# Where the 64-bit weight w_in is converted: in the first four chains, or beside the fifth chain and the first batch's V

## The chip, the cores and the metric

The kernel runs on one core of a Trainium2 chip. A core has five engines that follow instruction streams of their own and wait for one another by semaphores: TensorE (PE: matrix products, results in PSUM), VectorE (DVE), ScalarE (ACT), GpSimd (POOL) and SyncE (SP, which here only issues DMA transfers). Each engine works through its stream in order; a DMA is issued by one engine's queue and carried out by 16 DMA engines. The metric is the device time of one execution in microseconds (us).

## The reference

The reference has three stages on 4 batches of 768 positions. The first is a delta-rule attention with 8 heads of 48 channels; per head, with a 48x48 state:

```
y_t     = q_t @ state
state  += beta_t * outer(k_t, v_t - k_t @ state)      # k normalised
```

Its output x (4 x 768 x 384) goes through a gated MLP, in which w_in is float64:

```
h = gelu(x @ w_in);  u, v = h[..., :512], h[..., 512:]
v = w_sg @ layernorm(v) + b_sg                         # over positions
x = x + (u * v) @ w_out
```

and then through a token mixer and a channel MLP (two products with relu each, with w_tok1, w_tok2, w_ch1, w_ch2).

## The kernel before

**Stage one** (`phase_a`) turns the recurrence into blocks. It treats six groups g = 0..5, a group being two batches by a third of the positions. For each group there are these pieces:

- `kk(g)` and `qk(g)`: the products of keys with keys and queries with keys on TensorE (L159, L134), four units each. Their evictions go through ScalarE (L165, L169, L142); for g > 0 `kk` is then scattered into the tile MD by DMAs on SP's queue (L174, L175). GpSimd masks the query products (L145, L146).
- `solve(g)`: the inverse of a unit triangular matrix for 32 rows at a time, on VectorE: transpose MD into Li (L183), some scalars, 31 steps of a product and a sum (L209, L211), transposes into TD and TN (L214, L219). `tload` sends TD by four DMAs on SP's queue into the tile TW (L230).
- `merge(g)`: joins the blocks on TensorE with ScalarE evictions (L242 to L267). It waits for TW.
- `vput`: scaled values into YR on GpSimd (L273), which `chain` needs.
- `chain(g)`: the recurrence over four chunks c, four steps each, so 16 steps: `u` (L305), `d0`, `y0`, `y1` (L281, L291).

The order of instructions is written by hand. The six chains run one after the other; after each of a chain's 16 steps the table `ACT[g]` says what is put in: `S` advances solves, `K` and `Q` units of kk and qk, `m` units of merge, `l` the load of the next values, `v` the first `vput` of the next group, and `c` one step of a generator, `beside`, which converts w_in. Before the chains, the first solve runs through 31 steps `ns`, beside which ScalarE clears two AQ and one TW tile from the tile XZ (`zeros`, L108, L112): twelve pieces, four of them ahead of everything else, the rest from ns = 9 on.

**The conversion.** w_in arrives as pairs of 32-bit words. `load` works on tiles of 256 columns: a DMA on SP's queue into a tile `st` (L456); the square (`sq`, L468 on ScalarE or L469 on VectorE); four VectorE operations which build the float32 (`F`, L471, L472, L473, L476). `split` then makes a high and a low part, since the dense stages use three reduced-precision products in place of one float32 product (`mm3`, L547 to L549): a copy on ScalarE (L444), a subtraction on GpSimd (L445). With `out` given, the two parts are written to a DRAM buffer `scr` by two DMAs of GpSimd's queue (L487). Before, all 3072 columns (12 tiles) go this way while chains 0 to 2 run, with tiles of a pool of their own (`pcv`), which chain 3 gives back for the outputs xn of batches 2 and 3 (`room`).

**The dense stages** begin inside chain 5: its 16 steps each take one step of `pre`. `pre` loads the tile SA (named WIN) from `scr` by four DMAs on SP's queue (L699), transposes batch 0 (`trans`, L571 and L564), makes V (`V`, six blocks of 128 positions, evicted by gelu and layernorm, L577 to L593) and U (`U`, eight blocks). In this part two PSUM banks take turns, so a block's products wait until VectorE has read the block before the last one (L581). `start` sets up constants on GpSimd (L509 to L515). What is left of `pre` and the rest of the dense stages follow after chain 5.

Of the kernel before, what the change touches and what calls it, by code (L numbers as in the profile page):

```python
# [29 lines left out]
def phase_a(tc,I,xn,cfg,tail=None,beside=None,room=None):  # L30
    nc=cfg.get('wrap',lambda x:x)(tc.nc)
    es=ExitStack(); esE=ExitStack(); esP=ExitStack()
    with es:
# [80 lines left out]
        zs=zeros()  # L114
# [12 lines left out]
        def qk(g):  # L127
            for u in range(4):
# [7 lines left out]
                for par in range(2):  # L136
                    rr=T_[par]; q0=aq[rr,par].rearrange("p a c x -> p (a c) x")
                    if u in cfg['qd']:
                        nc.vector.tensor_tensor(q0,gp[rr],mask[rr].rearrange("p t x -> p (t x)").unsqueeze(1).to_broadcast([64,8,64]),ALU.mult)
                        continue  # L140
# [222 lines left out]
        for _ in range(4): next(zs)  # L363
# [7 lines left out]
        for ns in range(31):  # L371
# [4 lines left out]
            if ns>8: next(zs,0)  # L376
# [12 lines left out]
        vput(0,0)  # L389
        kt=[12]; mt=[8]  # L390
# [6 lines left out]
        for g in range(6):  # L397
# [4 lines left out]
            if g==3 and beside is not None:  # L402
                for _ in beside: pass
                room()
            if g==5 and tail is not None:
                while wait: tick()
                esP.close(); esE.close()
                fill=tail()
            for si,_ in enumerate(chain(g)):
                if fill is not None: next(fill,0)  # L410
                step[0]+=1; tick()
                for a in act[min(g,5)][si].split():
# [14 lines left out]
                    if a=='c' and beside is not None: next(beside,0)  # L427
# [6 lines left out]
def _dense(tc,I,O,xn,cfg):  # L434
# [11 lines left out]
    def load(src,hi,lo,parts,step=256,pool=None,ahead=2,g=1,out=None,lag=1):  # L446
# [33 lines left out]
        for i in range(0,n+lag*g,g):  # L480
            for j in range(max(i-lag*g,0),min(i-lag*g+g,n)):
                r=slice(todo[j][1],todo[j][1]+step)
                if out is None: split(Fs[j],hi[:,r],lo[:,r],True)
                else:
                    w=[pool.tile([128,step],F32R,name=n_,bufs=2) for n_ in ('sh','sl')]
                    split(Fs[j],w[0],w[1],True)
# [5 lines left out]
    def conv(PX,scr):  # L492

        yield from load(I['win'],None,None,[(0,3072,0)],pool=PX,lag=cfg.get('lag',1),g=cfg.get('cg',2),out=lambda r:(scr[0][:,r],scr[1][:,r]))
    me.conv=conv
    def start(scr):
# [199 lines left out]
        def pre():  # L696
            for h in (1,0):
                for i in range(2):
                    nc.sync.dma_start(R(WIN[i])[:,:,512*h:512*h+512],scr[i].rearrange("p (k f) -> p k f",f=1024)[:,:,512*h:512*h+512])  # L699
            yield from trans(0,XT)  # L700
            yield from V(0)
            yield from U(0)
# [84 lines left out]
def _row(ss,**k):  # L787

    r=[f'S{n}' if n else '' for n in ss]
    for a,at in k.items():  # L790
# [8 lines left out]
CFG={'nl':(0.5,0.2,0.7),'cg':2,'k0':(1,3,5,7),'q0':(11,13,15,17),'l1':20,'late':2,'far':3,'tl':2,'half':21,'hs':5,'qd':(),'act':ACT}  # L799
def build(tc,I,O,cfg):  # L800
    with tc.tile_pool(name="per",bufs=1,side="right") as pp, tc.tile_pool(name="scr",bufs=1,space=bass.MemoryType.DRAM) as pd, tc.manual_schedule():

        xn=[pp.tile([128,6,384],F32,name=f"xn{b}") for b in range(2)]
        d=_dense(tc,I,O,xn,cfg)
        scr=[pd.tile([128,3072],F32,name=f"scr{i}") for i in range(2)]
# [25 lines left out]
```

## Time and profile before

| | |
|---|---|
| median of 3 runs | 981.63 us (979.33 to 985.21) |
| profiled execution | 980.1 us, span 978.4 us |
| mean granted TensorE clock | 0.946 |
| PE busy | 856.8 us (88%) |
| DVE busy | 613.8 us (63%) |
| ACT busy | 391.2 us (40%) |
| POOL busy | 338.2 us (35%) |

A row of a timeline has the start and length in us, the engine, the line of the code, the instruction, its tiles (output <- inputs) and, in brackets, how long the engine had been idle before it and who released it. A row of the groups has the count, busy us, the mean ns of one, and idle time ahead. The chain of waits is followed back from the last instruction of the execution, and shown in order of time. DMA rows have the count, KB each and median us from issue to landing.

Stage one with the first steps of the dense stages takes the first third of the span (to about 340 us). The solves lie at 19 to 269 us, the chains at 78 to about 342, V of batch 0 at 308 to 330 on TensorE.

### The profile page before, as it was taken

The numbers are of one execution on the slowest core, as the hardware profiler recorded it, in microseconds if no ns is written. First come the engines' busy times: TensorE is split into PE (matmuls) and PEld (weight loads), VectorE is DVE, ScalarE is ACT, GpSimd is POOL, SyncE is SP. The second block draws the span as 40 slices with busy tenths as digits, with TensorE's granted clock in tenths as the row PEclk, the third lists the DMA queues.
The fourth block names the chain that finished last, engine by engine and source line by source line (L and its number), as shares of the span: only waits on it lengthen the run. The fifth ranks groups of instructions, "written<-read, shape, count | busy, mean of one in ns | idle before, by whom it ended". The sixth has DMA issues, their size and how long they took to land.

```text
span 978.4 us, 23130 instructions
## 1 busy us (share of the span) xinstructions
PE 856.8 (88%) x9644; PEld 812.9 (83%) x9644; DVE 613.8 (63%) x1254; ACT 391.2 (40%) x869; POOL 338.2 (35%) x434
## 2 busy tenths in 40 slices
PE   6456764878788899999999998989899999999998
PEld 4346764867787689999999987879899999999998
DVE  5999998989902787947839896878513213123122
ACT  4525543758787663423423432434212112112111
POOL 7330475777763534323234443834200000000000
PEclk9679776979999999999999997999999999999999
DMA  6564748675444040000000022224100000000000
GB/s 160 148 144 107 174 122 193 170 169 138 122 95 147 1 163 31 1 1 1 1 1 0 30 69 65 87 87 127 50 1 25 25 1 25 1 25 25 1 25 25
DMA packets 60344, 68.05 MB, mean 70 GB/s; under 512 B 30416, under 2 KB 37328, under 8 KB 60240
## 3 DMA queue, kind: packets, MB, share of 16 engines
q1 hardware_dynamic: 58288, 59.49, 23.3%
q0 software_dynamic: 1952, 7.08, 2.3%
q8 instruction: 76, 1.25, 0.5%
q14 instruction: 28, 0.23, 0.1%
HBM read 51.61 MB, written 7.86 MB: 61 GB/s over the span
## 4 chain that ended last, share of the span: by engine, by line
PE 65%; DVE 19%; ACT 4%; issue 4%; DMA 3%; POOL 2%; SPq 1%; DVEq 0%; ACTq 0%; POOLq 0%
PE ps L547 18%; PE ps L548 18%; PE ps L549 18%; DVE p L209 4%; DVE T L211 3%; DVE F L471 2%; DVE F L472 2%; DMA tw<-td 2%; PE yp L281 2%; PE gm L134 1%; PE gm L264 1%; PE ps L571 1%; DVE F L473 1%; PE ck L305 1%; PE gm L252 1%
## 5 line engine op out<-in xcount | busy, mean ns | idle before, releaser
L639 DVE SCALAR_TENSOR_TENSOR hlo<-ps,hh 128x384 fp32r<-128x384 f32 x96 | 53.5, 557 | 206.2 <-ACT hh L638 206.2
L638 ACT ACTIVATE hh<-ps 128x384 fp32r<-128x384 f32 x96 | 47.2, 491 | 227.1 <-PE ps L549 227.1
L547 PE MATMUL ps<-GU,SB 128*128 128x384 f32 x288 | 97.6, 339 | 0.0
L549 PE MATMUL ps<-GU,SB 128*128 128x384 f32 x288 | 97.5, 339 | 0.0
L548 PE MATMUL ps<-GU,SB 128*128 128x384 f32 x288 | 97.2, 338 | 0.0
L209 DVE TENSOR_TENSOR p<-Li,T 128x87 f32<-128x87 f32 (+15 forms) x186 | 81.2, 449 | 3.8
L211 DVE TENSOR_TENSOR T<-T,p 128x87 f32<-128x87 f32 (+15 forms) x186 | 74.2, 412 | 3.8
L548 PE MATMUL ps<-SB,VHt 128*128 128x384 f32 x192 | 65.0, 338 | 2.3 <-POOL SB L445 2.3
L549 PE MATMUL ps<-VHt,hlo 128*128 128x384 f32 x192 | 65.3, 340 | 1.3 <-DVE hlo L639 1.3
L547 PE MATMUL ps<-SB,VHt 128*128 128x384 f32 x192 | 65.0, 338 | 0.0
L547 PE MATMUL ps<-VHt,hh 128*128 128x384 f32 x192 | 65.0, 338 | 0.0
L548 PE MATMUL ps<-VHt,hh 128*128 128x384 f32 x192 | 64.6, 337 | 0.0
L549 PE MATMUL ps<-SB,VHt 128*128 128x384 f32 x192 | 64.5, 336 | 0.0
L614 POOL TENSOR_TENSOR q<-q,u 128x384 f32<-128x384 f32 x32 | 36.9, 1158 | 66.1 <-DVE q L613 66.1
L305 PE MATMUL ck<-yr,tw 128*64 128x48 f32 x768 | 38.1, 239 | 23.0 <-POOL yr L273 12.7
L273 POOL TENSOR_TENSOR yr<-v,nn 64x192 f32<-64x192 f32 x96 | 54.3, 566 | 9.0 <-DMA v<-in_vn_dram 2.2
L145 POOL TENSOR_SCALAR_AFFINE_SELECT aq<-aq 32x512 f32<-32x512 f32 x48 | 38.0, 791 | 55.6 <-ACT aq L142 50.7
L305 PEld LDWEIGHTS ck<-yr,tw 128*64 128x64 f32 x768 | 32.8, 151 | 26.8 <-POOL yr L273 14.7
L547 PE MATMUL ps<-X,SA 128*128 128x384 f32 x144 | 49.9, 346 | 5.8 <-DVE xn L626 3.2
L548 PEld LDWEIGHTS ps<-GU,SB 128*128 128x128 f32 x288 | 54.1, 188 | 0.9 <-DVE GU L564 0.9
L547 PEld LDWEIGHTS ps<-GU,SB 128*128 128x128 f32 x288 | 54.1, 188 | 0.6 <-DVE GU L564 0.6
L549 PEld LDWEIGHTS ps<-GU,SB 128*128 128x128 f32 x288 | 54.0, 188 | 0.3 <-POOL SB L445 0.3
(155 smaller groups left out, 2357.3 us busy)
## 6 DMA issues: line engine op xcount, KB each, us to landing
kq<-in_kq_dram SPq DMA_DIRECT2D x48, 256.0 KB, 4.3
st<-in_ch_dram SPq DMA_DIRECT2D x36, 256.0 KB, 2.8
aq<-in_qt_dram SPq DMA_DIRECT2D x24, 256.0 KB, 5.7
kn<-in_kn_dram SPq DMA_DIRECT2D x12, 384.0 KB, 7.0
out_dram<-xn SPq DMA_DIRECT2D x24, 192.0 KB, 1.9
v<-in_vn_dram POOLq DMA_DIRECT2D x10, 384.0 KB, 4.3
tw<-td SPq DMA_DIRECT2D x24, 128.0 KB, 4.3
st<-in_win_dram SPq DMA_DIRECT2D x12, 256.0 KB, 6.3
```

Source lines behind the costliest of these rows:

```text
L145: if blk==0: nc.gpsimd.affine_select(out=a,in_=a,pattern=[[0,8],[-64,2],[1,32]],compare_op=ALU.is_gt,fill=0.0,base=0,channel_multiplier=-1)
L209: nc.vector.tensor_tensor(p,Li[:,j,j+1:].unsqueeze(1).to_broadcast([128,w,n]),T[:,:w,j].unsqueeze(2).to_broadcast([128,w,n]),ALU.mult)
L211: nc.vector.tensor_tensor(T[:,:w,j+1:],T[:,:w,j+1:],p,ALU.add)
L273: n0=8*h+cc; nc.gpsimd.tensor_tensor(YRs[bb][gc%3][T_[par],:,par,:],VS[bb][T_[par],n0:n0+7:2,:],NNs[g%3][T_[par],16*bb+n0:16*bb+n0+7:2].un ...
L281: nc.tensor.matmul(yps[bb][o0:o0+64,2*pair+par,:],aq[F_,par,pair,cc,:],yr[F_,pair,par,:],start=True,stop=True)
L305: nc.tensor.matmul(u2[T_[par],pair,:],tw[F_,par,16*bb+8*h+2*pair+cc,:],yr[F_,pair,par,:],start=True,stop=True)
L547: nc.tensor.matmul(ps,L[0],Rr[0],start=first,stop=False)
L548: nc.tensor.matmul(ps,L[0],Rr[1],start=False,stop=False)
L549: nc.tensor.matmul(ps,L[1],Rr[0],start=False,stop=last)
L614: nc.gpsimd.tensor_tensor(gt,gt,u2[:,d,t],ALU.mult)
L638: nc.scalar.activation(hi,ps,AF.Relu)
L639: nc.vector.scalar_tensor_tensor(lo,ps,0.0,R(hi),op0=ALU.max,op1=ALU.subtract)
```

## The change

- The twelve tiles are no longer converted in chains 0 to 2. V's half of w_in (columns 512 to 1023 of each of three row blocks, six tiles) is converted in steps 8 to 15 of chain 4, two generator steps after each. It uses no pool: class `Spare` gives out parts of Li, MD, PP and T, whose last use is past by then. On this way the copy into the high part is on VectorE (`tensor_copy`), not on ScalarE. `scr` has half the columns.
- U's half (six tiles) is converted in `pre`, by the path that the other weights take: straight into SA, with the square and the copy on ScalarE, the subtraction on GpSimd. One step of it follows every second step of `trans` and of `V`; what is left comes ahead of `U`. `pre` loads only V's half from `scr`, by two DMAs.
- The pool `pcv` and `room` fall away; xn has four tiles from the start.
- The clearing pieces of `zeros` all run from ns = 1 on; none is put ahead of the first kk.
- One tile a time in place of two (`cg`) in the conversion to `scr`; an unused option (`qd`) is removed.

```
-                split(Fs[j],w[0],w[1],True)
+                nc.vector.tensor_copy(w[0],Fs[j]); nc.gpsimd.tensor_tensor(w[1],Fs[j],R(w[0]),ALU.subtract)
...
-        for _ in range(4): next(zs)
...
-            if ns>8: next(zs,0)
+            if ns>0: next(zs,0)
...
+        class Spare:
+            def __init__(self):
+                v=lambda t,o,n:t.rearrange("p a b -> p (a b)")[:,o:o+n]
+                self.b=dict(st=[v(Lis[0],0,512),v(Lis[0],512,512),v(MD,0,512)],F=[v(MD,512,256),v(MD,768,256)],
+                    sq=[PP[0][:,0:256]],sh=[v(Ts[0],0,256),v(Ts[0],256,256)],sl=[v(Ts[0],512,256),v(Ts[0],768,256)])
...
-            if g==3 and beside is not None:
-                for _ in beside: pass
-                room()
+            if g==4 and beside is not None: bs=beside(Spare())
             if g==5 and tail is not None:
                 while wait: tick()
+                for _ in bs: pass
...
-                    if a=='c' and beside is not None: next(beside,0)
+                    if a=='c':
+                        for _ in range(n_): next(bs,0)
...
-    def conv(PX,scr):
-        yield from load(I['win'],None,None,[(0,3072,0)],pool=PX,lag=cfg.get('lag',1),g=cfg.get('cg',2),out=lambda r:(scr[0][:,r],scr[1][:,r]))
+    def conv(scr,PX):
+        yield from load(I['win'],None,None,[(1024*k+512,1024*k+1024,512*k) for k in range(3)],pool=PX,out=lambda r:(scr[0][:,r],scr[1][:,r]))
...
         def pre():
-            for h in (1,0):
-                for i in range(2):
-                    nc.sync.dma_start(R(WIN[i])[:,:,512*h:512*h+512],scr[i].rearrange("p (k f) -> p k f",f=1024)[:,:,512*h:512*h+512])
-            yield from trans(0,XT)
-            yield from V(0)
+            for i in range(2): nc.sync.dma_start(R(WIN[i])[:,:,512:1024],scr[i].rearrange("p (k f) -> p k f",f=512))
+            ld=lw('win',WIN,[(1024*k,1024*k+512,1024*k) for k in range(3)])
+            yield from both(trans(0,XT),ld,cfg['u0'])
+            yield from both(V(0),ld,cfg['u1'])
+            for _ in ld: pass
             yield from U(0)
...
-ACT=[_row([3]*6+_st[6:],K=(3,4,6,7),Q=(9,10,12,13),c=(4,10,12,14),m=range(9,15),l=(9,),v=(15,),q=(14,)),
-     _row(_st,c=(1,4,7,9,12,15),z=(0,),**_k,**_m,**_s),_row(_st,c=(1,4,7,9,12,14),z=(0,),**_k,**_m,**_s),_row(_st,z=(0,),**_m,**_s),
+ACT=[_row([3]*6+_st[6:],K=(3,4,6,7),Q=(9,10,12,13),m=range(9,15),l=(9,),v=(15,),q=(14,)),
+     _row(_st,z=(0,),**_k,**_m,**_s),_row(_st,z=(0,),**_k,**_m,**_s),_row(_st,z=(0,),**_m,**_s),
...
+for i in range(8,16): ACT[4][i]+=' c2'
```

`both(a,b,n)` takes n steps of b for each step of a; `u0` and `u1` are 0.5.

More of the change, by code (lines that the diff above doesn't have):

```diff
@@ L28, in pack, with phase_a @@
     return dict(kq=half(tr(K)),qt=half(tr(Q)),vn=natv(V),kn=kn,bt=c(bt).reshape(2,3,128,32))
-def phase_a(tc,I,xn,cfg,tail=None,beside=None,room=None):
+def phase_a(tc,I,xn,cfg,tail=None,beside=None):
     nc=cfg.get('wrap',lambda x:x)(tc.nc)
@@ L137, in qk @@
                     rr=T_[par]; q0=aq[rr,par].rearrange("p a c x -> p (a c) x")
-                    if u in cfg['qd']:
-                        nc.vector.tensor_tensor(q0,gp[rr],mask[rr].rearrange("p t x -> p (t x)").unsqueeze(1).to_broadcast([64,8,64]),ALU.mult)
-                        continue
                     nc.scalar.copy(q0,gp[rr])
@@ L389, in phase_a, with tile @@
         vput(0,0)
+        class Spare:
[3 more added lines that the diff above has]
+                    sq=[PP[0][:,0:256]],sh=[v(Ts[0],0,256),v(Ts[0],256,256)],sl=[v(Ts[0],512,256),v(Ts[0],768,256)])
+                self.n={}
+            def tile(self,shape,dt,name,bufs=1):
+                b=self.b[name]; assert len(b)>=bufs,(name,bufs)
+                i=self.n[name]=self.n.get(name,-1)+1
+                x=b[i%bufs].bitcast(dt) if dt!=F32 else b[i%bufs]
+                return x.rearrange("p (a b) -> p a b",b=2) if len(shape)==3 else x
         kt=[12]; mt=[8]
@@ L795 @@
 _m=dict(m=(0,1,9,10,11,12,13,14)); _k=dict(K=(1,2,5,6))
-ACT=[_row([3]*6+_st[6:],K=(3,4,6,7),Q=(9,10,12,13),c=(4,10,12,14),m=range(9,15),l=(9,),v=(15,),q=(14,)),
-     _row(_st,c=(1,4,7,9,12,15),z=(0,),**_k,**_m,**_s),_row(_st,c=(1,4,7,9,12,14),z=(0,),**_k,**_m,**_s),_row(_st,z=(0,),**_m,**_s),
+ACT=[_row([3]*6+_st[6:],K=(3,4,6,7),Q=(9,10,12,13),m=range(9,15),l=(9,),v=(15,),q=(14,)),
+     _row(_st,z=(0,),**_k,**_m,**_s),_row(_st,z=(0,),**_k,**_m,**_s),_row(_st,z=(0,),**_m,**_s),
      _row([3]*9+[0]*7,z=(0,),m=(0,1,8,9,10,11,12,13,14,15),Q=(4,5,6,7),l=(9,),v=(15,)),_row([0]*16)]
-CFG={'nl':(0.5,0.2,0.7),'cg':2,'k0':(1,3,5,7),'q0':(11,13,15,17),'l1':20,'late':2,'far':3,'tl':2,'half':21,'hs':5,'qd':(),'act':ACT}
+for i in range(8,16): ACT[4][i]+=' c2'
+CFG={'nl':(0.5,0.2,0.7),'k0':(1,3,5,7),'q0':(11,13,15,17),'l1':20,'late':2,'far':3,'tl':2,'half':21,'hs':5,'u0':0.5,'u1':0.5,'act':ACT}
 def build(tc,I,O,cfg):
     with tc.tile_pool(name="per",bufs=1,side="right") as pp, tc.tile_pool(name="scr",bufs=1,space=bass.MemoryType.DRAM) as pd, tc.manual_schedule():
-        xn=[pp.tile([128,6,384],F32,name=f"xn{b}") for b in range(2)]
+        xn=[pp.tile([128,6,384],F32,name=f"xn{b}") for b in range(4)]
         d=_dense(tc,I,O,xn,cfg)
-        scr=[pd.tile([128,3072],F32,name=f"scr{i}") for i in range(2)]
-        with ExitStack() as es:
-            cv=es.enter_context(ExitStack())
-            PX=cv.enter_context(tc.tile_pool(name="pcv",bufs=2,side="right"))
-            def room():
-                cv.close()
-                P=es.enter_context(tc.tile_pool(name="per2",bufs=1,side="right"))
-                xn.extend(P.tile([128,6,384],F32,name=f"xn{b}") for b in (2,3))
-            phase_a(tc,I,xn,cfg,lambda:d.start(scr),d.conv(PX,scr),room)
-            d.rest()
+        scr=[pd.tile([128,1536],F32,name=f"scr{i}") for i in range(2)]
+        phase_a(tc,I,xn,cfg,lambda:d.start(scr),lambda P:d.conv(scr,P))
+        d.rest()
 def kernel(**inputs):
```

## The prediction

> **What bounds the kernel now.** I read four views in this order: the busy time of each engine by stretch, the chain of waits in order of time, the groups of instructions inside 95 to 225 us, and the instructions of single engines where the change puts work. Stretches first (PE, PEld, DVE, ACT, POOL busy us, then granted clock, DMA share, GB/s):
>
> ```profile
> 95.00:207.00 112.00, 78.04 (x2121) 73.39 (x2123) 105.01 (x239) 62.19 (x151) 68.88 (x106) 0.79 0.67 165
> 207.00:270.00 63.00, 48.62 (x1557) 45.71 (x1553) 58.56 (x115) 43.66 (x102) 47.69 (x78) 0.91 0.63 143
> 314.00:338.00 24.00, 19.17 (x198) 15.10 (x198) 21.09 (x38) 15.16 (x33) 11.67 (x15) 0.93 0.01 1
> ```
>
> VectorE is 94% busy from 95 to 207, so it looks like the bound where the conversion now lies. The chain of waits says otherwise (start, length, what):
>
> ```profile
> 123.89 0.53 POOL aq L146
> ...
> 124.50 0.76 POOL sl L445
> ...
> 127.08 1.05 POOL scr L487 x2
> ...
> 128.14 0.63 POOL yr L273
> ...
> 145.62 6.34 DMA kq<-in_kq_dram
> ...
> 158.02 8.59 DMA tw<-td
> ...
> 166.65 1.92 PE gm L242 x62
> ```
>
> From 95 to 207 the chain goes through TensorE, GpSimd's queue and transfers. VectorE has its part done before it is asked for, as two of its instructions show: the third solve's result is transposed at 149.15, but its transfer ends the wait only at 166.65; and the last solve's input at 207.21 finds VectorE waiting 2.21 us for a transfer.
>
> ```profile
> 149.15 2.08 DVE L214 STREAM_TRANSPOSE td<-T 128x1024 f32<-128x1024 f32 x1
> ...
> 207.21 1.95 DVE L183 STREAM_TRANSPOSE Li<-md 128x1024 f32<-128x1024 f32 x1 [2.21 <-DMA md<-gf]
> ```
>
> So taking work from VectorE there is not worth its busy time. It is worth what the same change takes from GpSimd's queue and from the transfers on that chain.
>
> **Removed: twelve tiles from the first chains.** The groups between 95 and 225 us:
>
> ```profile
> L469 DVE TENSOR_TENSOR sq<-st 128x256 f32<-128x256 f32 x12 | 6.3, 568 | 0.0
> L476 DVE SCALAR_TENSOR_TENSOR F<-sq,F 128x256 f32<-128x256 f32 x12 | 6.0, 540 | 0.0
> L473 DVE SCALAR_TENSOR_TENSOR F<-st,F 128x256 int32<-128x256 int32 x12 | 5.8, 521 | 0.0
> L472 DVE SCALAR_TENSOR_TENSOR F<-st,F 128x256 int32<-128x256 int32 x12 | 5.6, 506 | 0.0
> L471 DVE TENSOR_SCALAR F<-st 128x256 int32<-128x256 int32 x12 | 4.9, 447 | 0.0
> ...
> L445 POOL TENSOR_TENSOR sl<-F,sh 128x256 fp32r<-128x256 f32 x12 | 11.0, 920 | 18.8 <-issue 9.8 <-ACT sh L444 8.9
> L487 POOL DMA_DIRECT2D scr<-sh x12 | 6.8, 566 | 0.0
> L487 POOL DMA_DIRECT2D scr<-sl x12 | 6.5, 543 | 0.0
> ```
>
> VectorE loses 6.3 + 6.0 + 5.8 + 5.6 + 4.9 = 28.6 us, GpSimd 11.0 + 6.8 + 6.5 = 24.3 us, the DMA engines twelve loads and 24 stores. On the chain this is worth:
> - GpSimd: the two splits between 124.50 and 128.14 stand ahead of L273, for which TensorE waits: 128.14 - 124.50 = 3.6 us. Bounds: 2 (ScalarE's part ends then) and 5.
> - Transfers: the kq load takes 6.34 us and the tw load 8.59, while conversion loads and stores are in flight. Without them I let each take its median (the two rows below): 6.34 - 4.3 = 2.0 and 8.59 - 4.3 = 4.3, together 6.3 us. Bounds: 0 (their other neighbours, the kq, v and md loads, stay) and 8.
>
> ```profile
> kq<-in_kq_dram SPq DMA_DIRECT2D x48, 256.0 KB, 4.3
> ...
> tw<-td SPq DMA_DIRECT2D x24, 128.0 KB, 4.3
> ```
>
> SP's queue loses the twelve loads (L456) that stood between its kq, md and tw issues; that is part of the same 6.3 us.
>
> **Moved: the clearing of AQ and TW on ScalarE** (four pieces ahead of everything, the rest from step 9 on; now all from step 1 on). At the start the chain is:
>
> ```profile
> 7.01 1.99 ACT aq L108 x2
> 9.02 1.99 ACT aq L108 x2
> 11.02 0.36 ACT md L165
> ```
>
> TensorE's first products are there earlier:
>
> ```profile
> 7.23 2.09 PE L159 MATMUL gm<-kq 128*64 128x64 f32 x64
> ```
>
> Half of the 64 matmuls, the first eviction's, are done at 7.23 + 1.05 = 8.3, so ScalarE's L165 can start 11.02 - 8.3 = 2.7 us earlier; I take 2.6. What follows to the first solve hangs on it. Bounds: 1 and 3.5. The twelve pieces then lie on ScalarE beside the first solve, which is VectorE's; if that cover were gone, they would cost their 1 us each.
>
> **Added 1: V's six tiles in the fifth chain.** VectorE's six operations a tile cost nothing: it idles there (32.70 us ahead of the row below), and its st loads can go out as soon as SP has issued the last tw. If this cover were gone, six tiles by 28.6/12 = 2.4 us would be 14 us. GpSimd's queue is the price. Its six subtractions and twelve stores stand behind the v load and ahead of the first yr of the sixth chain, for which L305 waits:
>
> ```profile
> 289.09 1.11 POOL L79 DMA_DIRECT2D v<-in_vn_dram  x2
> 292.42 2.25 POOL L273 TENSOR_TENSOR yr<-v,nn 64x192 f32<-64x192 f32 x4 [2.22 <-DMA v<-in_vn_dram]
> ```
> ```profile
> 298.26 1.11 PE L305 MATMUL ck<-yr,tw 128*64 128x48 f32 x31
> ```
> ```profile
> 301.52 0.56 DVE L564 TENSOR_TENSOR X<-ps,X 128x384 fp32r<-128x384 f32 x1 [32.70 <-ACT X L564]
> ```
>
> A split takes 0.76 + 0.57 + 0.54 = 1.87 us. Its buffers sh and sl are two each, so the third and the fifth split wait until the store of the one two before has landed. Landings of sl's stores and, second line, of the SA loads:
>
> ```profile
> DMA to landing us min/median/max: 2.1/4.1/7.6
> ```
> ```profile
> DMA to landing us min/median/max: 6.2/8.4/10.4
> ```
>
> The DMA engines are nearly empty there, so I take 2.1: two splits cost 0.76 + 1.11 + 2.1 = 4.0, the six end at 290.2 + 4.0 + 4.0 + 3.7 = 301.9, half of L273's four (1.1) is done at 303.0, and L305 starts 303.0 - 298.3 = 4.7 us later. The setting up of the sixth chain (idt, gh, bh) and its second yr stand behind that in GpSimd's queue and move along. Bounds: 2.8 (some 2 us of small waits of TensorE up to 308 take it in) and 8.7 (landing 4.1: 2.0 more at each of the two waits).
>
> Then V's weights: the last store lands at 301.9 + 2.1 to 4.1 = 304.0 to 306.0, SA's two loads some 7 us later, at 311 to 313. V's first matmul, now at 308.44, would stand at 313.1: just met. The first st load of U's half queues behind SA's on SP and is awaited on VectorE ahead of the last X pieces: 1.0 us, bounds 0 and 3. Sum for the fifth chain: 5.7 us.
>
> **Added 2: U's six tiles beside the first batch.** VectorE has 21.09 us of work in the 24 us from 314 to 338, and TensorE waits for it:
>
> ```profile
> 308.44 0.50 PE L547 MATMUL ps<-SA,X 128*128 128x512 f32 x1
> ...
> 334.23 0.44 PE L547 MATMUL ps<-X,SA 128*128 128x384 f32 x1 [2.11 <-DVE q L581]
> ```
> ```profile
> 311.44 0.69 DVE L578 SCALAR_TENSOR_TENSOR q<-q,ps 128x512 f32<-128x512 f32 x1 [2.10 <-ACT q L577]
> 314.44 0.69 DVE L581 SCALAR_TENSOR_TENSOR q<-q,ps 128x512 f32<-128x512 f32 x1 [2.31 <-ACT q L580]
> ...
> 358.06 0.28 DVE L471 TENSOR_SCALAR F<-st 128x256 int32<-128x256 int32 x1
> ...
> 359.71 0.29 DVE L471 TENSOR_SCALAR F<-st 128x256 int32<-128x256 int32 x1
> ...
> 361.79 0.29 DVE L471 TENSOR_SCALAR F<-st 128x256 int32<-128x256 int32 x1
> ...
> 363.87 0.29 DVE L471 TENSOR_SCALAR F<-st 128x256 int32<-128x256 int32 x1
> ```
>
> The same code on w_out shows a tile's step: 359.71 - 358.06 = 1.65 us alone, 363.87 - 361.79 = 2.08 beside GpSimd's subtraction. Tiles 0 and 1 fall into the gaps of 2.10 and 2.31 us. Tiles 2 to 5 stand between V's evictions and those of U, which give the two PSUM banks back: four by 1.85 (between the two steps) = 7.4 us. Afterwards TensorE is the bound, and nothing gives it back. Bounds: 3 (the last two in U's gaps) and 12.5 (six by 2.08).
>
> [...]
>
> **Sum.** Removed 3.6 + 6.3 + 2.6 = 12.5; added 5.7 + 7.4 = 13.1; net +0.6 us. The profiled execution took 980.1 us (span 978.4), so 980.7; the median of the runs is 1.5 above it: **982**. Two large amounts cancel, and either may be off by five.
>
> **Rivals.**
> 1. VectorE does set the pace of the first chains. For it: 105.01 of 112 us. Against it: the two waits shown first. About half of the 28.6 us lies ahead of the transpose at 149.15. If the first stretch follows VectorE, 14.3 takes the place of 9.9 (-4.4); if the second does, 14.3 - 2.2 = 12.1 more; the middle is -8.3: 974. Both together would be 966.
> 2. The transfers do not shorten. The tw pieces and the kq, v and md loads beside them stay, and a transfer that is only among these is as long as before: the 6.3 us fall away, 988. For it: SP issues these in a row. Against it: both were far above their median.
> 3. V's weights come late (slower). The place is the row of last store, landing, SA load. At the median landing the splits end at 301.9 + 4.0 = 305.9, the store lands at 310.0, SA 8.4 us later at 318.4: 10.0 us after 308.44 instead of 5.7, and with SA's longest landing (10.4) 12.0. That is +4.3 to +6.3: 987. It decides once that row ends after 313 us of the old clock.
> 4. The change doesn't do what it says: only if the dead tiles are not dead when SP reaches the loads. VectorE, their last reader, is done by 301.52 - 32.70 = 268.8, so I leave it without a chance.
>
> **Chances.** Forecast 0.44, rival 1 0.28, rival 2 0.14, rival 3 0.14. 0.5% is 4.9 us, about what a measurement of this kernel can tell from no change. Rival 1 is faster by more than that, with 0.04 of the forecast's own spread: 0.32. Rivals 2 and 3 mostly slower, 0.23, with 0.03 of the forecast: 0.26. Same: 0.42. The forecast alone would run from 976 to 987; the range takes in most of the rivals: 968 to 989.
>
> **What would show it.** Right: L165's first copy near 8.4; the tw transfer of the third solve near 4 us; VectorE's last solve input about 12 us earlier, with VectorE idle ahead of it; GpSimd's six splits back to back ahead of L273; L305 of the sixth chain waiting for that yr; V's six evictions some 7 us longer in all. Wrong: a last solve input 20 us or more earlier, or V's start waiting for SA, or V no longer than before.

## The result and the profile after

The changed kernel took 999.21 us (median of 4 runs, 993.40 to 1000.57), and the kernel before took 983.42 us beside it (4 runs, 979.33 to 988.99). The ratio is 1.0149, with a 95% interval of 1.0108 to 1.0189: 14.7 us slower. The prediction was 982 us with a range of 968 to 989, so the result lies outside the range on the slow side. The ratios of all runs leave out executions in a slower state, among them two of the ten of run 7 (1632 and 1635 us), whose cause is not known.

| | before | after |
|---|---|---|
| profiled execution | 980.1 us, span 978.4 | 1000.6 us, span 998.8 |
| mean granted TensorE clock | 0.946 | 0.920 |
| third solve's result transposed (VectorE) | 149.15 | 137.80 |
| sixth merge's first products (TensorE) | 279.80 | 275.79 |
| sixth chain's first 32 products | 298.26 | 300.54 |
| V's first product | 308.44 | 315.52 |
| U's second block | 334.23 | 350.29 |

So a lead of 4.0 us at the sixth merge becomes a loss of 2.3, then 7.1, then 16.1 us. Most of the 20.4 us between the two spans arises between 276 and 350 us. The code's lines have moved: L305 is now L302, L273 is L270, L242 is L239, L230 is L227, L547 is L555, L581 is L589.

**First chains** (0 to 2, where the conversion was). The busy time by stretch of the kernel after (columns as in the prediction):

```profile
95.00:200.00 105.00, 74.97 (x2144) 70.36 (x2144) 76.57 (x178) 60.07 (x143) 54.59 (x78) 0.83 0.54 129
```

VectorE had 105.01 us of work in 112 us before; it now has 76.57 in 105. Single instructions of VectorE, SP's queue and TensorE in the kernel after:

```profile
137.80 2.14 DVE L211 STREAM_TRANSPOSE td<-T 128x1024 f32<-128x1024 f32 x1
...
150.58 4.72 SPq L227 DMA_DIRECT2D tw<-td  x4
...
161.21 1.91 PE L239 MATMUL gm<-tw,G 128*32 128x32 f32 x62 [6.00 <-DMA tw<-td]
...
198.70 1.95 DVE L180 STREAM_TRANSPOSE Li<-md 128x1024 f32<-128x1024 f32 x1 [10.17 <-DMA md<-gf]
```

and the row of SP's queue in the kernel before that answers to the second one:

```profile
156.62 4.95 SPq L230 DMA_DIRECT2D tw<-td  x4
```

The last solve's input comes 8.5 us earlier (the prediction had said about 12), and VectorE has then been idle for 10.17 us, which the prediction had asked for. But the third solve's transfer is no shorter. From SP's issue to the end of TensorE's wait it took 166.65 - 156.62 = 10.0 us before and takes 161.21 - 150.58 = 10.6 us now.

**Fifth chain.** GpSimd's instructions of the kernel after, from the load of the last values on:

```profile
283.15 1.11 POOL L79 DMA_DIRECT2D v<-in_vn_dram  x2
284.32 0.72 POOL L494 TENSOR_TENSOR T<-md,T 128x256 fp32r<-128x256 f32 x1
...
289.84 0.84 POOL L494 TENSOR_TENSOR T<-md,T 128x256 fp32r<-128x256 f32 x1 [1.96 <-DVE T L494]
...
298.18 0.72 POOL L494 TENSOR_TENSOR T<-md,T 128x256 fp32r<-128x256 f32 x1 [0.90 <-DVE T L494]
298.84 1.10 POOL L495 DMA_DIRECT2D scr<-T  x2
299.96 1.10 POOL L270 TENSOR_TENSOR yr<-v,nn 64x192 f32<-64x192 f32 x2
```

VectorE's in the same stretch, and TensorE's first products of the sixth chain:

```profile
285.08 0.29 DVE L479 TENSOR_SCALAR md<-md 128x256 int32<-128x256 int32 x1 [3.98 <-POOL T L494]
...
289.46 0.29 DVE L494 CAST T<-md 128x256 fp32r<-128x256 f32 x1 [1.86 <-DMA scr<-T]
...
292.24 0.29 DVE L494 CAST T<-md 128x256 fp32r<-128x256 f32 x1
...
297.80 0.29 DVE L494 CAST T<-md 128x256 fp32r<-128x256 f32 x1
...
300.54 2.83 PE L302 MATMUL ck<-yr,tw 128*64 128x48 f32 x32 [7.25 <-POOL yr L270]
```

The six splits with their twelve stores occupy GpSimd's queue from 284.32 to 299.94, 15.6 us, ahead of the `yr` for which TensorE stands idle for 7.25 us. They are not back to back. VectorE has two tiles ready, then waits for GpSimd's first split (3.98 us) and for a store to land (1.86). From 289.46 on it works without a pause, one copy every 2.78 us up to 297.80, and GpSimd, which needs 1.9 us for a split and its stores, waits some 0.9 us for each. After that gap the clock is low (stretches of the kernel after):

```profile
296.00:298.00 2.00, 0.00 (x0) 0.00 (x0) 1.86 (x5) 0.00 (x0) 1.28 (x3) 0.50 0.27 94
...
302.00:304.00 2.00, 1.93 (x22) 1.48 (x19) 0.00 (x0) 1.14 (x4) 0.77 (x4) 0.50 0.34 54
...
316.00:318.00 2.00, 2.00 (x6) 1.52 (x6) 1.68 (x4) 0.00 (x0) 0.26 (x1) 0.50 0.01 4
318.00:320.00 2.00, 2.00 (x25) 1.30 (x25) 0.00 (x0) 0.38 (x1) 0.00 (x0) 0.68 0.42 131
```

In the kernel before, the whole stretch ran at a clock of 1.00:

```profile
280.00:330.00 50.00, 42.97 (x936) 35.62 (x929) 17.73 (x32) 36.45 (x85) 26.43 (x45) 1.00 0.26 89
```

**V.** The chain of waits of the kernel after, in order of time:

```profile
301.72 0.52 POOL yr L270
302.28 1.09 PE ck L302 x14
...
314.56 1.03 PE yp L278 x16
315.59 0.72 PE ps L555
...
325.66 0.21 DVE F L479
...
327.30 0.42 DVE F L484
...
333.84 0.55 DVE F L479
...
335.88 1.32 DVE F L484
...
343.89 0.21 DVE F L479
...
347.60 0.44 DVE F L484
...
348.06 0.41 ACT SA L452
```

From 302.28 to 315.59 it is TensorE's own work alone, at a granted clock of 0.50. In V it runs through VectorE's conversion of four of U's six tiles (F, L479 to L484): 325.66 to 327.72, 333.84 to 337.20, and the last two one behind the other, 343.89 to 348.04. These are 2.1 + 3.4 + 4.1 = 9.6 us, 2.4 a tile. ScalarE's copy of the last one into SA follows. The first two tiles were converted at 311.50 to 317.86, before V's first eviction, and are not on the chain.

### The profile page after: what moved, and what is told of

It is laid out like the page before. It is cut to its first block, busy times and chain, and to the rows that moved or that the text cites. A ratio compares the mean times of both kernels' runs of the same rounds, so it can differ in the third digit from the quotient of the medians.

```text
span 998.8 us, 23103 instructions
## 1 busy us (share of the span) xinstructions
PE 870.9 (87%) x9643; PEld 825.3 (83%) x9644; DVE 610.5 (61%) x1254; ACT 391.3 (39%) x869; POOL 336.2 (34%) x422
## 4 chain that ended last, share of the span: by engine, by line
PE 57%; DVE 9%; ACT 2%; issue 1%; POOL 1%; DMA 0%; DVEq 0%; POOLq 0%; ACTq 0%
PE ps L555 18%; PE ps L556 18%; PE ps L557 18%; DVE F L479 2%; DVE F L480 2%; PE ps L579 2%; DVE F L481 1%; DVE F L484 1%; PE yp L278 1%; DVE q L621 0%; DVE xn L634 0%; ACT SB L452 0%; DVE q L589 0%; PE ck L302 0%; POOL VHt L453 0%
## 5 line engine op out<-in xcount | busy, mean ns | idle before, releaser
L555 PE MATMUL ps<-GU,SB 128*128 128x384 f32 x288 | 98.7, 343 | 0.0
L206 DVE TENSOR_TENSOR p<-Li,T 128x87 f32<-128x87 f32 (+15 forms) x186 | 75.7, 419 | 4.0
L142 POOL TENSOR_SCALAR_AFFINE_SELECT aq<-aq 32x512 f32<-32x512 f32 x48 | 41.0, 855 | 83.7 <-ACT aq L139 59.3
L555 PE MATMUL ps<-SB,VHt 128*128 128x384 f32 x192 | 65.5, 341 | 0.0
L555 PE MATMUL ps<-VHt,hh 128*128 128x384 f32 x192 | 65.0, 338 | 0.0
L270 POOL TENSOR_TENSOR yr<-v,nn 64x192 f32<-64x192 f32 x96 | 58.3, 607 | 7.0
L302 PE MATMUL ck<-yr,tw 128*64 128x48 f32 x768 | 39.4, 247 | 22.2 <-POOL yr L270 11.8
L555 PE MATMUL ps<-X,SA 128*128 128x384 f32 x144 | 50.9, 353 | 7.5 <-DVE xn L634 3.2
L302 PEld LDWEIGHTS ck<-yr,tw 128*64 128x64 f32 x768 | 34.0, 160 | 26.5 <-POOL yr L270 14.0
L556 PEld LDWEIGHTS ps<-GU,SB 128*128 128x128 f32 x288 | 54.9, 191 | 0.7 <-DVE GU L572 0.7
L555 PEld LDWEIGHTS ps<-GU,SB 128*128 128x128 f32 x288 | 55.0, 191 | 0.5 <-DVE GU L572 0.5
L557 PEld LDWEIGHTS ps<-GU,SB 128*128 128x128 f32 x288 | 54.8, 190 | 0.3 <-POOL SB L453 0.3
```

What stands on the lines that cost most here:

```text
L142: if blk==0: nc.gpsimd.affine_select(out=a,in_=a,pattern=[[0,8],[-64,2],[1,32]],compare_op=ALU.is_gt,fill=0.0,base=0,channel_multiplier=-1)
L206: nc.vector.tensor_tensor(p,Li[:,j,j+1:].unsqueeze(1).to_broadcast([128,w,n]),T[:,:w,j].unsqueeze(2).to_broadcast([128,w,n]),ALU.mult)
L270: n0=8*h+cc; nc.gpsimd.tensor_tensor(YRs[bb][gc%3][T_[par],:,par,:],VS[bb][T_[par],n0:n0+7:2,:],NNs[g%3][T_[par],16*bb+n0:16*bb+n0+7:2].un ...
L302: nc.tensor.matmul(u2[T_[par],pair,:],tw[F_,par,16*bb+8*h+2*pair+cc,:],yr[F_,pair,par,:],start=True,stop=True)
L555: nc.tensor.matmul(ps,L[0],Rr[0],start=first,stop=False)
L556: nc.tensor.matmul(ps,L[0],Rr[1],start=False,stop=False)
```

## The experiments

Ratios are to the kernel before, run beside on the same chip, with 95% intervals; 1% is 9.8 us. Instants are those of the profiled executions, and single executions scatter: the change, run 4 and run 13, whose code is the same up to there, reach the sixth merge at 275.79, 276.60 and 282.12. Lengths inside one execution say more than instants.

**1 to 3. Each part alone.** The part that isn't converted is filled from a DRAM buffer with values of x instead of w_in, at the same point and with as many loads into SA; the dense stages then compute with these values. The fifth chain's conversion or the one beside V is taken out. The six stores that fill this buffer stand where V's conversion would be; in run 2 they come behind its last tile.

```
-        yield from load(I['win'],None,None,[(1024*k+512,1024*k+1024,512*k) for k in range(3)],pool=PX,out=lambda r:(scr[0][:,r],scr[1][:,r]))   # nothing, U alone
+        w=PX.tile([128,256],F32R,name='sh',bufs=2); nc.vector.tensor_copy(w,xn[0][:,0,0:256])
+        for i in range(6): nc.sync.dma_start(me.raw[:,256*i:256*i+256],R(w))
...
-            ld=lw('win',WIN,[(1024*k,1024*k+512,1024*k) for k in range(3)])   # nothing, V alone
+            for i in range(2): nc.sync.dma_start(R(WIN[i])[:,:,0:512],me.raw.rearrange("p (k f) -> p k f",f=512))
+            ld=iter(())
```

> The changed kernel without any conversion of w_in: both halves of SA are loaded from a buffer that holds other numbers, by four loads as before (the result is not the reference's). This is what the removal and the earlier clearing are worth by themselves. Theory (the traces of before and after: the fifth chain's last chunk starts 4.9 us earlier, and nothing is added): 974 to 979, about 6 us under before. Rival, the sum of the prediction (12.5 us removed): 970 or less. Rival, the first chains are bound by transfers and give nothing back: within 2 us of before.

> The changed kernel with V's half converted in the fifth chain and U's half not converted (loaded from a buffer with other numbers; the result is not the reference's). Theory: the wait for GpSimd's yr at the start of the sixth chain stands with its 7 us idle TensorE and the low granted clock behind it; about 10 us over the run without conversion. Rival (the prediction's term, 5.7 us): about 6 over it. If the two parts only hurt together: 2 or less.

> The changed kernel with U's half converted beside V and V's half not converted (its part of SA loaded from a buffer with other numbers; the result is not the reference's). Theory: VectorE's four tiles between V's evictions, 8 to 9 us over the run without conversion, with the granted clock at 1.0 at V's start. Rival (it is the low clock that made V long): 4 or less.

| | ratio | median us | sixth chain's 32 | V's first | U's second block |
|---|---|---|---|---|---|
| nothing converted | 0.9925 [0.990, 0.995] | 976.3 | 291.52 | 301.68 | 327.46 |
| V's half alone | 1.0059 [1.0019, 1.0098] | 991.4 | 305.39 | 320.09 | 345.88 |
| U's half alone | 1.0072 [1.0032, 1.0111] | 989.3 | 290.30 | 303.21 | 337.67 |
| both (the change) | 1.0149 [1.0108, 1.0189] | 999.2 | 300.54 | 315.52 | 350.29 |

What the removal brings is 0.0075 by 983 = 7.4 us, not the 12.5 of the prediction. V's half costs 0.0134, 13.2 us, on top of that; U's half 0.0147, 14.4 us; each of these differences is uncertain by some 5 us (half the intervals, 0.0025 and 0.0040, added as squares). Beside the other one V's half costs 7.6 us and U's half 8.9: what the two cost together, 22.1 us, is less than 13.2 + 14.4 = 27.6, by about as much as is uncertain. Run 1 lies in its expected range; runs 2 and 3 cost more than expected (about 10, and 8 to 9 us).

Run 2 holds something that the change does not. Its chain of waits goes through the stores of the buffer, for which the loads of the dense stages' constants then wait:

```profile
303.93 0.33 SPq L504
...
306.31 2.34 DMA raw<-T
...
309.35 3.61 DMA bh<-in_b_dram
```

So part of the 13.2 us may be the buffer's, and the 8.9, which is taken against run 2, may be too small. The 14.4 and the 7.6 have no such stores on their way.

Lengths inside the executions separate the halves further. From V's first product to U's second block it is 25.8 us before, with nothing converted and with V's half alone, 34.5 with U's half alone and 34.8 with both. So V is 8.7 to 9.0 us longer wherever U's half is converted beside it. From the 32 products to V's first product it is 10.2 us before and with nothing converted, and 12.9 with U's half alone. There the chain of waits goes through U's first load, which queues behind the loads of SA:

```profile
291.88 7.62 DMA st<-in_win_dram
```

The clock, which was expected to stay at 1.0, is at 0.50 from about 299.5 to 306 in that run, behind an idle time of 1.28 us; its mean from 295 to 340 is 0.78. Rows of SP's queue and of TensorE with nothing converted:

```profile
147.65 4.78 SPq L227 DMA_DIRECT2D tw<-td  x4
...
158.10 1.92 PE L239 MATMUL gm<-tw,G 128*32 128x32 f32 x62 [5.11 <-DMA tw<-td]
```

Even with no conversion transfer anywhere in these chains, the third solve's transfer takes 158.10 - 147.65 = 10.5 us until TensorE goes on. In these traces its length does not depend on the conversion.

**4. Filler products in the gap.** 28 products of 128x512 bf16 at the end of the fifth chain, where TensorE is idle before `yr`.

```
+ACT[4][15]+=' W28'
```

> The changed kernel with 28 products of zeros (128x128 by 128x512, bf16) on TensorE at the end of the fifth chain, in the 7.25 us in which it waits for GpSimd. Theory: the granted clock stays near 1.0 from 300 to 319 in place of 0.50, and V starts about 3 us earlier; 3 to 5 us under the changed kernel. Rival (the clock goes low for another reason, or the time is set by GpSimd, VectorE and the transfers): no change within 1 us.

The ratio is 1.017 [1.0115, 1.0225], 1001.0 us: no gain. TensorE was idle for 1.40 us after the filler, and the clock fell to 0.50 from 304 to 313 all the same, so this run didn't test what it was made for (run 13 does).

**5. GpSimd out of V's conversion.**

```
-nc.vector.tensor_copy(w[0],Fs[j]); nc.gpsimd.tensor_tensor(w[1],Fs[j],R(w[0]),ALU.subtract)
-for x,y in zip(out(r),w): nc.gpsimd.dma_start(x,R(y))
+nc.vector.tensor_copy(w[0],Fs[j]); nc.vector.tensor_tensor(w[1],Fs[j],R(w[0]),ALU.subtract)
+for x,y in zip(out(r),w): nc.sync.dma_start(x,R(y))
```

> The changed kernel with GpSimd taken out of the conversion of V's half: in the fifth chain VectorE makes the subtraction too (six more operations of 0.3 to 0.8 us beside VectorE's idle time of 254 to 272), and SP's queue instead of GpSimd's stores the 12 halves. U's half stays beside the first batch's V. Theory (the price of V's half is GpSimd's queue: six splits and twelve stores of 0.55 us in front of the last beta times v, so that TensorE stood idle for 7.25 us): the sixth chain's first product of 32 starts at 290 to 293 as in the kernel with U's half alone (290.3), the first product of V before 305, no stretch of clock 0.50 longer than 10 us around 300, and the time is that of the kernel with U's half alone, 987 to 991. Rival (the price is the late weights or the converting as such, wherever it is done): first product of V at 312 or later and a time of 995 to 1000.

1.0099 [1.0066, 1.0131], 992.4 us. This is 0.0050, 4.9 us, under the change (uncertain by 5) and 2.7 above U's half alone. The sixth chain's 32 products start at 294.42 without a gap of 7 us ahead of them, and the median lies a little above the theory's range. V's first product is at 309.77, not before 305. VectorE's rows say what came in its place:

```profile
306.08 0.58 DVE L479 TENSOR_SCALAR F<-st 128x256 int32<-128x256 int32 x1 [4.72 <-DMA st<-in_win_dram]
...
308.25 0.56 DVE L572 TENSOR_TENSOR X<-ps,X 128x384 fp32r<-128x384 f32 x1
```

U's first tile is awaited for 4.72 us on VectorE, and the last two evictions of x transposed (L572) stand behind it. It is the wait which the prediction had put at 1.0.

**6. The same work, another order.** On GpSimd's queue the last `yr` stands ahead of the splits. In this order it overwrites values which the fifth chain still uses, so part of that chain's output is not the reference's.

```
-for i in range(8,16): ACT[4][i]+=' c2'
+ACT[4][15]=ACT[4][15].replace('v','').strip()
+ACT[4][10]+=' v'
+for i in range(11,16): ACT[4][i]+=' c4'
```

> The changed kernel with one thing in another order: on GpSimd's queue the last beta times v of the sixth chain stands ahead of the six splits and twelve stores instead of behind them (the conversion is issued from row 11 of the fifth chain, four steps a row). All operations are the same. Theory: the sixth chain's 32 products start at 291 to 294 (300.5 in the changed kernel) and TensorE has no gap of 7 us ahead of them, but the six splits now begin some 4 us later on GpSimd, so that the stores, the weights and the first product of V come at 308 to 314: the price moves from the queue to the weights, and the time is 990 to 997. Rival A (the queue's order is the whole price): first product of V at 303 to 305, 987 to 991. Rival B (the order is indifferent): 997 to 1001.

1.0121 [1.0052, 1.0190], 999.5 us, a miss; the median is in the range of rival B. TensorE has the same gap in an earlier place, since its products now wait for the new contents of the buffer:

```profile
287.65 1.45 PE L278 MATMUL yp<-yr,aq 128*64 128x48 f32 x14 [7.52 <-POOL yr L270]
```

It leaves open what the order alone is worth.

**7. The clearing alone.** The kernel before with its zeroing moved as in the change.

```
-        for _ in range(4): next(zs)
...
-            if ns>8: next(zs,0)
+            if ns>0: next(zs,0)
```

> The kernel before with one part of the change alone: the zeroing of the solve buffers is taken from ahead of the loads and spread over the first solve's steps, so that the first copies start earlier. The conversion stays in the first four chains. The prediction put 2.6 us on this. Theory now (the first solve ends some 4 us earlier, but its result waits on SP's queue behind the loads of q and k, and the first merge's products start at the same time as before): first transposition of the first solve some 4 us earlier (19.2 to about 15), first merge's products within 1 us of 62.1, ratio 0.999 to 1.001. Rival (the prediction's step): ratio 0.996 to 0.998.

0.9991 [0.9958, 1.0024]: no change is seen, though 2.6 us (0.0026) would still lie inside the interval. The trace says more. VectorE, SP's queue and TensorE in this run:

```profile
15.52 1.98 DVE L183 STREAM_TRANSPOSE Li<-md 128x1024 f32<-128x1024 f32 x1
...
54.10 6.97 SPq L230 DMA_DIRECT2D tw<-td  x4
...
62.77 1.44 PE L242 MATMUL gm<-tw,G 128*32 128x32 f32 x46 [0.87 <-DMA tw<-td]
```

The same row of SP's queue in the kernel before:

```profile
56.36 4.12 SPq L230 DMA_DIRECT2D tw<-td  x4
```

The first solve starts 19.24 - 15.52 = 3.7 us earlier and its transfer is issued 2.3 earlier. But the issue of the four pieces, behind the loads of queries and keys, takes 6.97 us instead of 4.12, and the first merge's products start at 62.77 instead of 62.09. In this trace the gain ends in SP's queue.

**8 and 12. V's half on VectorE in the fifth chain, U's half in the first three chains as before.** In run 12 the last solve's instructions are also written out at the head of the fifth chain, so that the first loads of w_in stand ahead of its transfer on SP's queue.

```
 # 8, against the kernel before: six tiles in chains 0 to 2, six in the fifth chain
-        yield from load(I['win'],None,None,[(0,3072,0)],pool=PX,lag=cfg.get('lag',1),g=cfg.get('cg',2),out=lambda r:(scr[0][:,r],scr[1][:,r]))
+        yield from load(I['win'],None,None,[(1024*k,1024*k+512,1536+512*k) for k in range(3)],pool=PX,lag=cfg.get('lag',1),g=cfg.get('cg',2),out=lambda r:(scr[0][:,r],scr[1][:,r]))
...
+            if g==4: bs=beside2(Spare())
...
+for i in range(8,16): ACT[4][i]+=' c2'
 # 12, against 8
-            if g==4: bs=beside2(Spare())
+            if g==4: bs=beside2(Spare()); adv(62); next(bs)
...
-for i in range(8,16): ACT[4][i]+=' c2'
+for i in range(1,8): ACT[4][i]+=' c2'
```

> A kernel between the two: V's half is converted in the fifth chain, all of it on VectorE and stored by SP's queue; U's half stays in the first three chains as before (six tiles there instead of twelve, splits on GpSimd). Beside V nothing is converted. The zeroing stands at the start as in the kernel before. Theory (the fifth chain's VectorE has the room, and the first chains pay 7.4 us for twelve tiles): the sixth chain's 32 products follow without a long gap, V has no conversion of 2.5 to 3.4 us in it, and the time is 979 to 982, 2 to 4 us under the kernel before, and 7 to 10 under the changed kernel with GpSimd taken out. Rival (the removal pays only when the first chains hold no conversion at all): 983 to 986.

> The kernel between the two (U's half in the first three chains, V's half in the fifth chain on VectorE, stored by SP's queue), with V's half begun earlier as in the run before: the first loads of w_in for it ahead of the last solve's transfer. Theory (the version with V's half begun at 276 lost its 10 us in the sixth chain since the last store and the loads behind it came at 298 to 310): V's first product at 302 to 307 instead of 312.9, 978 to 983, ratio 0.992 to 0.998. Rival (the sixth chain begins when the fifth chain's loads and the last solve's transfer are there, and these come later by what is put ahead of them): first product of V at 309 or later, 984 to 989.

1.0018 [0.9988, 1.0049] and 1.0013 [0.9977, 1.0049]: neither differs from the kernel before, and both theories missed (run 12's rival, 309 or later and 984 to 989, was right). V's first product is at 312.90 in the one and, though its conversion was begun earlier, at 315.20 in the other. What half of the conversion may bring when it is taken from the first chains is lost again by V. The two also warn against single traces. Up to the fifth chain their code is the same, yet the fifth solve's result is transposed at 222.62 in the one profiled execution and at 235.86 in the other.

**9. All twelve tiles in the fifth chain, on VectorE, begun early.**

```
+            if g==4 and beside is not None: bs=beside(Spare()); adv(62); next(bs)
...
 # within the arguments of load:
-    [(1024*k+512,1024*k+1024,512*k) for k in range(3)]
+    [(1024*k+o,1024*k+o+512,512*k+1536*j) for j,o in enumerate((512,0)) for k in range(3)]
...
-for i in range(8,16): ACT[4][i]+=' c2'
+for i in range(1,16): ACT[4][i]+=' c2'
...
 # subtraction and stores as in run 5; nothing converted beside V
```

> All twelve tiles are converted in the fifth chain, V's six first, all on VectorE, stored by SP's queue; nothing in the first chains and nothing beside V. The last solve's instructions are written out at the head of the fifth chain, so that the first three loads of w_in stand on SP's queue ahead of the loads and of the transfer that took until 268 in the changed kernel, and VectorE begins to convert at 252 to 255 instead of 272. Theory (what costs in the fifth chain is GpSimd's queue and the lateness of loads and weights, not VectorE's work, which has 40 us of idle time from 254 to 294 without a conversion; twelve tiles of 2.7 to 4.5 us make 32 to 54): V's first product at 302 to 308, nothing converted in V, and a time of 977 to 982, ratio 0.993 to 0.998 to the kernel before. Rival 1 (VectorE's tiles are not done by 295 and the evictions of x transposed wait behind them): first product of V at 310 or later, 984 to 990. Rival 2 (VectorE's operations beside GpSimd's selects slow the fifth chain itself): the sixth chain's 32 products at 296 or later, 983 to 988.

1.0063 [1.0030, 1.0095], 991.5 us, a miss. The signs of both rivals are there (V's first product at 320.83, the 32 products at 299.52), and the time lies above both their ranges. VectorE began at 263.29, not at 252 to 255, and was done at 307.3. A row of GpSimd:

```profile
309.58 0.10 POOL L517 MEMSET mh<- 128x1 f32 x1 [14.59 <-DMA scr<-T]
```

The dense stages' constants take the memory of the dead tiles, so GpSimd waits for the last store to land before it sets them up, and the sixth chain's `yr` stands behind that. V itself then takes no longer than with nothing converted (25.8 us to U's second block in both).

**10. One VectorE operation instead of four for each of U's tiles.** To the kernel with U's half alone; the two words of w_in are not put together, so that U's half of the weight is not w_in.

```
+            if one:
...
+                    nc.vector.scalar_tensor_tensor(Fs[i],sq[j],THR*THR,w[j][:,:,1].bitcast(F32),op0=ALU.is_ge,op1=ALU.mult)
+                return
```

> The kernel with U's half converted beside V and V's half not converted at all, with one thing less: of VectorE's four operations for each of the six tiles of U's half only the last is left (the two words are not put together; the half of w_in is not the reference's). Loads, ScalarE's square and copy and GpSimd's subtraction stay. Theory (VectorE sets V's pace, and the four operations of 2.0 to 3.0 us a tile are the price): U's second block of products 5 to 8 us earlier than 337.7, at 329 to 333, and 979 to 984 (989.3 with four operations, 976.3 with none). Rival (the price is in the loads, ScalarE, GpSimd or the granted clock): U's second block at 335 or later, 987 to 990.

0.9963 [0.9934, 0.9993], 982.2 us: 0.0109, 10.7 us (uncertain by 5), under the kernel with four operations, though loads, ScalarE's and GpSimd's parts are all there. U's second block is at 334.17 (337.67 with four, 327.46 with none), later than the theory had it, but the time is inside its range. From V's first product to that block it is 29.1 us, against 34.5 with four operations and 25.8 with none: three operations take 5.3 of the 8.7 us there. VectorE's groups from 296 to 350 us with four operations:

```profile
L480 DVE SCALAR_TENSOR_TENSOR F<-st,F 128x256 int32<-128x256 int32 x6 | 3.6, 595 | 0.2
L484 DVE SCALAR_TENSOR_TENSOR F<-sq,F 128x256 f32<-128x256 f32 x6 | 3.4, 574 | 0.6
L481 DVE SCALAR_TENSOR_TENSOR F<-st,F 128x256 int32<-128x256 int32 x6 | 3.4, 574 | 0.2
L479 DVE TENSOR_SCALAR F<-st 128x256 int32<-128x256 int32 x6 | 2.3, 389 | 2.3 <-DMA st<-in_win_dram 2.3
```

These are 3.6 + 3.4 + 3.4 + 2.3 = 12.7 us, 2.1 a tile, and 2.3 us of waiting for the tiles' loads.

**11. The changed kernel's conversion, begun early.** All operations on their engines as in the change.

```
+            if g==4 and beside is not None: bs=beside(Spare()); adv(62); next(bs)
...
-for i in range(8,16): ACT[4][i]+=' c2'
+for i in range(1,8): ACT[4][i]+=' c2'
```

> The changed kernel, all its operations and their engines as they are (GpSimd makes the six splits and issues the twelve stores), with V's half begun earlier: the last solve's instructions are written out at the head of the fifth chain and the conversion from its second row, so that the first loads stand on SP's queue ahead of the transfer of the last solve, and the splits lie between GpSimd's selects of 265 to 285 instead of in one row from 284 to 300. Theory (the price of V's half is its place, behind the last loads and in one row ahead of beta times v, not its work): the sixth chain's 32 products at 291 to 296 (300.5 in the changed kernel), no gap of 7 us ahead of them, V's first product at 303 to 308, and 988 to 993. Rival (the work itself on GpSimd, some 11 us, is the price wherever it lies): the sixth chain's products at 298 or later, 995 to 1000.

1.0173 [1.0108, 1.0237], 999.9 us: the rival was right. GpSimd's splits now lie between its selects, from 261.84 to 291.4, and delay the selects, the load of the last values and another `yr`. TensorE and GpSimd in this run:

```profile
291.98 2.73 PE L302 MATMUL ck<-yr,tw 128*64 128x48 f32 x31 [5.53 <-POOL yr L270]
```
```profile
293.60 1.12 POOL L79 DMA_DIRECT2D v<-in_vn_dram  x2
```

The load of the last values is issued at 293.60 (283.15 in the change), the gap is 5.53 us instead of 7.25, the sixth chain's 32 products start at 302.67, and V's first product is at 316.41. So GpSimd's work in this chain, six times a split of 0.7 to 0.8 us and two stores of 1.1 together, some 11 us, costs in both places where it was put.

**13. Filler products up to the end of the gap.** As run 4, with 37.

```
+ACT[4][15]+=' W37'
```

> The changed kernel with 37 filler products of 128x512 bf16 on TensorE at the end of the fifth chain in place of 28: at 0.22 us each they last 8.2 us and reach to where beta times v of the sixth chain lets TensorE go on, so that no idle time of 1.4 us is left between them and the 32 products, as there was with 28. Nothing else is changed. Theory (after the gap the granted clock of 0.50 lengthens TensorE's own work up to V's first product, which took 15.0 us from the 32 products on in the changed kernel and 10.2 in the kernel before): the clock is 0.9 or more from 303 to 318, V's first product follows within 11 us of the 32 products, and the time is 994 to 997. Rival (the weights and GpSimd's setting up set V's start, or the clock falls without idle time too): V's first product 14 us or more after the 32 products, 998 to 1002.

1.0195 [1.0156, 1.0234], 1005.0 us, above the ranges of theory and rival. The clock was up, at 1.00 to 315 and at a mean of 0.90 from there to 320:

```profile
305.00:310.00 5.00, 4.87 (x50) 2.55 (x48) 0.00 (x0) 0.47 (x2) 3.77 (x10) 1.00 0.27 64
310.00:315.00 5.00, 4.47 (x67) 3.48 (x68) 2.02 (x4) 3.84 (x11) 3.25 (x4) 1.00 0.99 329
```

and from the 32 products at 308.73 to V's first at 320.59 TensorE took 11.9 us, against 15.0 in the change and 10.2 before. So with the clock up 3.1 of these 4.8 us are gone in this trace. The rest became other waits: GpSimd's next `yr` behind its setting up of the dense stages, and ScalarE behind the load of U's first tile.

```profile
317.31 0.43 ACT L476 ACTIVATE sq<-st 128x256 f32<-128x256 f32 x1 [2.69 <-DMA st<-in_win_dram]
```

In the time nothing was gained. The filler ended 1.6 us after GpSimd had the `yr` ready (305.98 + 1.1 = 307.1), and this profiled execution was already late at the sixth merge, 282.12 instead of 275.79.

## Why the prediction was wrong

1. **What bounds the first chains.** The two waits it read were real. The last solve's input comes earlier, by 8.5 us and not by 12, and after a long idle time of VectorE. Taking the work away brought 7.4 us (run 1) of the 12.5 forecast, and rival 1, in which VectorE sets the pace (8.3 us more than the sum's 12.5), is out.
2. **The step "Transfers: 6.3 us" failed.** It let two transfers shrink to their median. The third solve's took 10.0 us before, 10.6 after and 10.5 with no conversion at all. This was rival 2: the runs show that the transfer stays as long among its neighbours, but not what sets its length there. The other one, the kq load (2.0 of the 6.3 us), does not stand on the chain of waits of run 1. The median of a group does not say what a transfer takes between its neighbours.
3. **The step "clearing moved: 2.6 us" failed, by the trace.** The first copy came even earlier than said (7.54 instead of 8.4), but in run 7 the first merge starts no earlier than before: the transfer at the other end of the first solve gives the gain back. The time of run 7 alone would not exclude 2.6 us. With 2 and 3 at nothing, the 7.4 us are more than the 3.6 put on GpSimd's splits. How they divide between GpSimd's queue and VectorE's 28.6 us was not separated.
4. **The step "Added 1: 5.7 us" had the right mechanism, GpSimd's queue, but two of its terms failed.** That the queue is the main price is what run 11 and the gap in the trace say, and run 5 as far as its interval allows. The first failed term is "VectorE's six operations a tile cost nothing: it idles there". With two buffers VectorE can be only two tiles ahead of GpSimd; from the third tile on its own 2.78 us a tile set the pace, not GpSimd's 1.9. The six splits took 15.6 us, not 290.2 to 301.9 = 11.7. The lead of 4.9 us at the fifth chain's last chunk (289.30 to 284.41) became a delay of 2.3: 7.2 us in place of 4.7. The second is the clock of 0.50 behind the gap of 7.25 us, which was left out: from the 32 products to V it is 15.0 us in place of 10.2, and 3.1 of these 4.8 us are absent in the trace with the clock up (run 13, whose time was no shorter). In the change V does not wait for its weights, so rival 3 did not occur as written. With GpSimd out of the way, its neighbour did: U's first load was awaited for 4.72 us (run 5). V's half costs 7.6 us beside U's half, which can't be told from 5.7; alone it was 13.2, with the buffer's stores of run 2 in it.
5. **The step "Added 2: 7.4 us" was too small.** VectorE's operations are the main price (run 10: 10.7 us for three of the four). Four tiles are on the chain, as it said, but they take 2.4 us each there, not 1.85. In the change's trace V to U is 16.1 - 7.1 = 9.0 us longer. In the time U's half alone costs 14.4; there its first load also delays V by 12.9 - 10.2 = 2.7 us, where the prediction had put 1.0. Over all six tiles VectorE was busy 2.1 a tile (run 3), and no run tested what lengthens the four on the chain.
6. **The sum.** Removal -7.4, V's half +13.2, U's half beside it +8.9; or removal -7.4, U's half +14.4, V's half beside it +7.6. Both give the measured +14.7, since they are differences of the same four times. The second order has no buffer's stores on its way. The prediction had -12.5, +7.4 for U's half and +5.7 for V's. So the two halves cost 22.1 us where it had 13.1, and the removal brought 7.4 where it had 12.5. Both errors point the same way, where it had thought that they may cancel.

## What to carry to other kernels

Work that is taken from a busy engine is worth what the chain of waits gives back after the next queue (here 7.4 us for 28.6 us of VectorE's work and 24.3 of GpSimd's), and a transfer's length between its neighbours is to be read where it stands (8.59 us on the chain of waits before), not taken from the median of its group (4.3). An engine that is idle is only half of a free place: here VectorE had been idle for 32.70 us before the change, but each of its tiles also needed GpSimd, where the six splits and their stores took 15.6 us ahead of the instruction that TensorE waits for. The idle engine's work was not free either: with two buffers between them, VectorE and GpSimd went from the third tile on at the pace of the slower one, VectorE's 2.78 us a tile, not GpSimd's 1.9. The gap of 7.25 us on TensorE had a clock of 0.50 behind it, which belongs into such an estimate too (15.0 us in place of 10.2 until V), though the higher clock of run 13 brought nothing in the time, since other waits took its place.

## What the runs showed that was not expected

**The clock after a gap.** In the change TensorE was idle from 293.3 to 300.5, and the granted clock was 0.50 from 295.5 to 319.0, though TensorE was busy 1.93 to 2.00 of every 2 us from 302 on. In these traces neither the length of an idle time nor that of the work behind it says alone what the clock does. In the change the clock is at 1.00 up to 295.0 and at 0.50 from 295.5, some 2 us into the idle time. In run 4 it fell behind idle times of 1.40 and 0.27 us, in run 3 behind one of 1.28; in the kernel before it fell behind one of 2.11 us (work again from 334.23, 0.50 from 335.0), but stayed at 1.00 behind idle times of 1.43 (work again from 294.97) and 1.64 (from 326.37). The return took some 18 us of work in the change, about 7 in run 11 (work again from 292, 0.50 to 298, 1.00 from 300) and about 4 in the kernel before (1.00 from 338.5). What else decides isn't known from these runs.

**A long select on GpSimd.** Of the selects on 32x512 elements, which take 0.7 to 1.0 us, one took 4.35 in the profiled execution of the kernel after, while VectorE worked without a pause on two solves (18.83 of 19 us):

```profile
217.28 4.35 POOL L142 TENSOR_SCALAR_AFFINE_SELECT aq<-aq 32x512 f32<-32x512 f32 x1
```
```profile
213.00:232.00 19.00, 15.14 (x409) 14.24 (x410) 18.83 (x50) 12.29 (x27) 17.66 (x24) 0.82 0.63 143
```

These 4.35 us are longer than any single VectorE instruction from 213 to 224 (at most 1.12); what lengthened the select was not shown. It is not tied to the change: eight of the fifteen traces have one such select of 3.6 to 4.4 us, and run 4 and run 13, whose code is the change's up to there, have none. So single executions differ by up to 3.6 us in this one instruction; no run tested what that costs in the time.
